# Four small reorderings in a spectral filter fused with a feed-forward layer: x's split, a DFT, a weight buffer and the first PSUM pools

## The chip, the cores and the metric

The kernel runs on one core of a Trainium2 chip. The metric is the device time of one launch in microseconds (us); the times given are medians of several runs. Engines are named as in the profile: PE is TensorE (PEld its weight loads), DVE is VectorE, ACT is ScalarE, POOL is GpSimd, and SP issues every DMA from one queue in order. Each engine works through its own instructions in the order in which the program issues them.

## The reference

Eight batches of 3008 x 256 are transformed along the sequence, mixed by a complex linear layer, shrunk towards zero and transformed back; the result, as 24064 tokens, passes a feed-forward layer of width 2048 with the activation h - tanh(h).

```python
X = np.fft.rfft(x, axis=1)
Yr = Xr @ w_r - Xi @ w_i + b_r
Yi = Xr @ w_i + Xi @ w_r + b_i
Yr = np.sign(Yr) * np.maximum(np.abs(Yr) - lam, 0.0)      # the same for Yi, lam = 0.01
y = np.fft.irfft(Yr + 1j * Yi, n=x.shape[1], axis=1)
h = y.reshape(B * S, D) @ w_in                            # w_in 256 x 2048
out = (h - np.tanh(h)) @ w_out                            # w_out 2048 x 256
```

## The kernel before

**Precision.** Most operands are kept as a high and a low part (hi rounded to the fp32r format by ACT, lo the difference, by POOL or DVE): `split_into`, line 87 for ACT's cast and 88 for the subtraction. A product is then three matmuls: low x high, high x high, high x low. So a matmul group needs its second operand's low half only at its third step.

**The transforms.** 3008 = 64 x 47, so each DFT is done in two steps with a trip through DRAM between them. `Forward` does the first step: `load` brings a piece of x, `split` (a cast x_h on ACT, a subtraction x_l on POOL), `part` (three matmuls, lines 216 to 218, and a copy `st` on ACT that a DMA stores to `a`). `Spectrum` does the rest for a pair of frequencies: `load` reads `at` from `a`; `dft` (line 262) is the second DFT step, with two copies on ACT and two operations on DVE; `shared` and `cross` are the linear layer's products into `ps_t` and `ps_v` (line 289); `join` makes `tb` from `ps_t` (line 300) and then `y` from `tb` and `ps_v` (line 326); `shrink` is the shrinkage; `inverse` (lines 336 to 338) the first step back, with a copy `zo` on ACT that is stored to `z`. `Unit` reads `zin` from `z` and does the last step (line 428) into `raw`, a chunk of 512 or 480 tokens.

**The feed-forward layer.** Chunks 0 to 2 go through `rise`/`fall` directly (H or he, line 481; down, line 505). From chunk 3 on, w_in's product is done as a seven-product 2 x 2 scheme: `Pair` computes two of 16 feature blocks at a time into H in four phases, from sums of weights (`sums`, made once by `weight_sums`) and from sums of halves of the chunk (`sums` and `operands` of `Chunk`; names t1 to t4 and b11 to b22; tiles `y_t`, `y_b`, and `y_more` for b22 and t4). DVE's `u3` (line 592) and `low_right` (line 598) work inside H between the phases. Then tanh (607), the difference (610), the split into gh (614) and gl (618), and the product with w_out (505).

**Order.** All five engines follow the order written in the program (`manual_schedule`). From chunk 3 on a period Q handles one Pair; it has two slots, sa = 46 + 2Q and sb = 47 + 2Q, into which everything else is planned ahead of time. An event in a slot has a rank; `run(slot)` issues them in order of rank, then of insertion. What an event returns is issued later (`run_later`, `run_last`, in the next period's beginning or after the slot). Ranks before: 0 loads, 1 `operands`, 2 `Forward.split`, `shrink` (which only returns its work) and `inverse`, 3 `cross`, 4 `shared`, 6 `dft`, 7 `Forward.part`, 8 `Unit.time`, 9 `Chunk.sums` and `weight_step`.

For a chunk whose first period begins at slot zs, `prepare` puts the operands t3, b11, t2 and b21 into slot zs-3, t1 into zs-2, b22 and t4 into zs-1. Batch 1's spectrum starts at slot 56 with a new pair every 2 slots: dft at k, shared and cross at k+1, shrink at k+2, inverse at k+4. So from slot 60 to 78 every even slot holds one pair's dft and another pair's inverse. Other batches have a pair every 6 slots, and their dft and inverse fall into slots of different parity. The first DFT step of batch b from 2 on is put into the 16 calmest of 20 slots, `split` one slot ahead of its `part`. The weight sums take four steps for each of four parts, in slots 36 to 43 and 46 to 53.

**PSUM** has eight banks. At the start there are three pools: ps_h (2 banks), ps_o (2) and ps_f (4). They are closed together, and ps_oo (2), ps_ff (2) and ps_e (4: he0, he1, oe0, oe1) take their banks in this order. `bank(...)` gives a bank of ps_f first, of ps_ff from then on; from that point ps_f1, ps_f2, ps_t1, ps_v, ps_i1 and ps_i2 all come from its two banks. A new pool waits for the readers and writers of the old pools that lie under it, unless it is opened with `reuse_waits="tile"`, in which case each tile waits only for those under the tile. Later ps_H (two tiles of two banks) takes the banks of ps_e in that way.

Of the kernel before, what the change touches and what calls it, by code (L numbers as in the profile page):

```python
# [10 lines left out]
F32 = mybir.dt.float32  # L11
# [3 lines left out]
ALU = mybir.AluOpType  # L15
# [6 lines left out]
def index_maps():  # L22
    n = np.arange(S)
    time = np.zeros((64, 47), np.int64)
    time[n % 64, n % 47] = n
    starts = []
    for j in range(NJ):
        low = (47 * np.arange(64) + 64 * j) % S < S // 2
        starts.append(next(m for m in range(64) if low[m] and not low[m - 1]))
    return time, starts  # L30
# [36 lines left out]
def spectral_ffn(ctx, tc, x, w_r, w_i, b_r, b_i, w_in, w_out, f1, f2, i1, i2, out):  # L67
    nc = tc.nc
    P = 128
    w_in, w_out = w_in.bitcast(U32), w_out.bitcast(U32)  # L70
    _, m0 = index_maps()
    CT = 512
    NF = FF // P
    PSUM = bass.MemoryType.PSUM
# [3 lines left out]
    work = ctx.enter_context(tc.tile_pool(name="work", bufs=2))  # L78
    ffn = ctx.enter_context(tc.tile_pool(name="ffn", bufs=2))
    dram = ctx.enter_context(tc.tile_pool(name="dram", bufs=2, space=bass.MemoryType.DRAM))  # L80
    start = ExitStack()
    ps_h = start.enter_context(tc.tile_pool(name="ps_h", bufs=2, space=PSUM))
    ps_o = start.enter_context(tc.tile_pool(name="ps_o", bufs=1, space=PSUM))
    ps_f = start.enter_context(tc.tile_pool(name="ps_f", bufs=4, space=PSUM))

    def split_into(hi, lo, src, rest=nc.gpsimd):
        nc.scalar.copy(out=hi, in_=src)  # L87
        rest.tensor_tensor(out=lo, in0=src, in1=hi.bitcast(F32), op=ALU.subtract)  # L88
        return hi, lo
# [149 lines left out]
    def rows(t, jp):  # L239
        return t.rearrange("a (g j) d -> a g (j d)", j=NJ)[:, :, 2 * jp * D:(2 * jp + 2) * D]  # L240

    class Spectrum:
# [98 lines left out]
        def put(self, pz):  # L341
            zo = work.tile([P, 512], F32, name="zo", tag="tmp", bufs=4)
            nc.scalar.copy(out=zo, in_=pz)
            nc.sync.dma_start(out=rows(z_dram[self.b], self.jp), in_=zo)
# [60 lines left out]
    def h(t):  # L405
        return t.bitcast(F32)
# [215 lines left out]

    def weight_sums(p):
        wv = [w.rearrange("p k (q i m) -> p k i q m", i=2, m=P)[:, :, :, 2 * p:2 * p + 2] for w in (win_h, win_l)]
        t = [work.tile([P, 2, P], F32, name=f"ws{k}", tag="tmp", bufs=4) for k in range(3)]

        def whole(dst, k, i):
            nc.vector.tensor_tensor(out=dst, in0=h(wv[0][:, k, i]), in1=h(wv[1][:, k, i]), op=ALU.add)

        def op(dst, a, b, how):  # L630
            nc.vector.tensor_tensor(out=dst, in0=a, in1=b, op=how)

        def put_sum(i, src):
            split_into(*(v[:, 2 * p * P:(2 * p + 2) * P].rearrange("p (q m) -> p q m", m=P) for v in sums[i]), src)

        def one():
            whole(t[0], 0, 1)
            whole(t[2], 0, 0)
            whole(t[1], 1, 1)

        def two():
            op(t[1], t[0], t[1], ALU.add)
            op(t[0], t[2], t[0], ALU.subtract)
            put_sum(2, t[0])

        def three():
            put_sum(0, t[1])
            op(t[1], t[1], t[2], ALU.subtract)
            whole(t[2], 1, 0)

        def four():
            put_sum(1, t[1])
            op(t[2], t[2], t[1], ALU.subtract)
            split_into(wv[0][:, 0, 1], wv[1][:, 0, 1], t[2])

        return one, two, three, four

    slots = {}
# [4 lines left out]
    later = [[], []]  # L663

    def run(slot):
        for _, _, fn, a in sorted(slots.pop(slot, []), key=lambda e: e[:2]):
            later[0].extend(fn(*a) or ())

    def run_later():
# [18 lines left out]
    def busy(slot, us):  # L688
        load_at[slot] = load_at.get(slot, 0.0) + us

    def plan_spectrum(b, at, each, offsets, ahead, earliest):
        shared, cross, shrink, inverse = offsets
        done_at[b] = at + (NJ // 2 - 1) * each + inverse
        for jp in range(NJ // 2):
            s = Spectrum(b, jp)
            k = at + jp * each
            put(max(k - ahead, earliest), 0, s.load)
            for slot, rank, fn, us in (
                (k, 6, s.dft, 1.8), (k + shared, 4, s.shared, 0.7), (k + cross, 3, s.cross, 1.4),
                (k + shrink, 2, lambda s=s: [s.shrink], 0.3), (k + inverse, 2, s.inverse, 0.7),  # L700
            ):
                put(slot, rank, fn)
                busy(slot, us)
            if shared == cross:
                busy(k + shared, 9.0)

    def plan_forward(f, q, slot):
        put(slot - 1, 2, f.split, q)
        put(slot, 7, f.part, q)
        busy(slot, 0.8)  # L710
        busy(slot - 1, 0.1)
# [21 lines left out]
    def plan():  # L733
# [8 lines left out]
        for ch in range(LOOK, NP // XC):  # L742
            k = ch - LOOK
            f = following[ch]
            put((40, 41, 44, 47, 48, 49)[k], 0, f.load)
            for q in range(XC // 2):
                plan_forward(f, q, 47 + k)
        plan_spectrum(1, 56, 2, (1, 1, 2, 4), 5, 53)
        for b in range(2, B):
            zs = zero_slot(b * WB_N)  # L750
            plan_spectrum(b, zs - 89, 6, (2, 3, 4, 7), 7, zs - 92)
        for b in range(2, B):
            zs = zero_slot(b * WB_N)
            at = calmest(zs - 113, zs - 94, NP // 2, 0.8)
            for ch in range(NP // XC):
                f = Forward(b, ch)
                put(at[2 * ch] - 5, 0, f.load)
                for q in range(XC // 2):
                    plan_forward(f, q, at[2 * ch + q])
# [13 lines left out]
    def weight_step(p, k):  # L773
        if not sums:
            sums.extend([piece(i + 3 * v, [P, FF // 2], F32R, f"sum{i}_{v}") for v in range(2)] for i in range(3))
        if k == 0:
            wsteps[p] = weight_sums(p)
        wsteps[p][k]()
# [27 lines left out]
    with tc.manual_schedule(engines={E.PE, E.Activation, E.DVE, E.Pool, E.SP}):  # L806
# [24 lines left out]
        for i in range(len(steps) + 2):  # L831
# [9 lines left out]
            if i >= 2:  # L841
                f, q = steps[i - 2]
# [120 lines left out]
        ps_ff = ctx.enter_context(tc.tile_pool(name="ps_ff", bufs=2, space=PSUM))  # L963
        banks[0] = ps_ff
        first_pass = ExitStack()
        ps_e = first_pass.enter_context(tc.tile_pool(name="ps_e", bufs=1, space=PSUM))
        early_h = [ps_e.tile([P, 512], F32, name=f"he{k}", tag=f"he{k}") for k in range(2)]
        early_o = [ps_e.tile([P, 512], F32, name=f"oe{k}", tag=f"oe{k}") for k in range(2)]
        H = []
# [35 lines left out]
        for g in range(-AHEAD, LAST):  # L1005
            rise(g + AHEAD)
            if g < CONV:
                early(g)
                if g == CONV - 1:
                    some(80)  # L1010
                    assert raw_count == 16 and not any(pending) and not any(streams)
                    plan()
            else:
                run(g)
                run_later()
                run_last()
            finish(g + AHEAD)
            for t in range(2):
                fall(g, t)
# [14 lines left out]
        for Q in range(-1, PERIODS + 2):  # L1034
# [13 lines left out]
            call(Q + 1, "keep")  # L1048
            run_last()
            run(sa)  # L1050
            run_later()
            finish(sa + AHEAD)
# [10 lines left out]
            fall(sb, 0)  # L1063
            call(Q - 1, "down", 0, 0)
            run(sb)
            fall(sb, 1)
            call(Q - 1, "down", 0, 1)
# [34 lines left out]
```

## Time and profile before

| | |
|---|---|
| median of 3 runs | 2660.9 us (2659.74 to 2662.64) |
| profiled execution | 2656.65 us; span from first to last instruction 2654.8 us |
| PE busy | 2611.6 us, 98% |
| DVE, ACT, POOL busy | 65%, 59%, 26% |
| mean granted PE clock | 0.994 |
| HBM read and written | 86.13 and 74.97 MB |

The span less PE's busy time is the time in which PE stood still. A row of the wait list names who waited, for whom, for how long in total, how often, and the longest time. In the timeline a row gives start and duration in us, engine, line, operation, the tile written and the tiles read, how many instructions were merged, and in brackets the idle time ahead of it and what ended it. A merged row's duration reaches to the end of its last matmul; matmuls overlap, so the next one starts before.

### The profile page before, as it was taken

How to read it: one execution, taken by the hardware profiler on the slowest of the kernel's cores; microseconds unless marked ns; L12 is line 12 of the kernel's file. 1: busy time of each engine (PE TensorE's matmuls, PEld its weight loads, DVE VectorE, ACT ScalarE, POOL GpSimd, SP SyncE). 2: the span in 40 equal slices, each digit the busy share in tenths (PEclk: the TensorE clock that was granted, in tenths of full speed). 3: DMA queues.
4: the chain of work that ended last, by engine and by line, in shares of the span. 5: the costliest groups of instructions: out<-in, count | busy, mean ns of one | idle time of the engine just before them, and what ended most of it. 6: DMA issues, size and time to landing. Idle time of an engine off the chain costs nothing.

```text
span 2654.8 us, 43312 instructions
## 1 busy us (share of the span) xinstructions
PE 2611.6 (98%) x16641; PEld 2343.2 (88%) x16641; DVE 1720.6 (65%) x2613; ACT 1578.9 (59%) x2950; POOL 697.9 (26%) x829
## 2 busy tenths in 40 slices
PE   8999999999999999999999999999999999999999
PEld 6787788899989999899998999989999899999998
DVE  6787676576656667466664666646665566665655
ACT  5555656655566555755566555665556655555555
POOL 0002524322242222512334232332223322221210
PEclk8899999999999999999999999999999999999999
DMA  6420313211131111311114011231112211111000
GB/s 195 149 76 14 110 59 102 70 40 53 38 111 55 47 50 40 106 59 40 45 49 125 29 54 38 73 95 41 43 52 84 68 46 55 36 33 33 16 24 16
DMA packets 104654, 163.90 MB, mean 62 GB/s; under 512 B 8000, under 2 KB 62272, under 8 KB 104352
## 3 DMA queue, kind: packets, MB, share of 16 engines
q1 hardware_dynamic: 104448, 161.13, 19.7%
q8 instruction: 132, 2.16, 0.3%
q14 instruction: 74, 0.61, 0.1%
HBM read 86.13 MB, written 74.97 MB: 61 GB/s over the span
## 4 chain that ended last, share of the span: by engine, by line
PE 86%; DVE 2%; POOL 1%; ACT 1%; issue 1%; DMA 0%; SPq 0%; POOLq 0%; ACTq 0%; DVEq 0%
PE o L505 36%; PE H L576 32%; PE ps_v L289 4%; PE ps_i L428 4%; PE ps_f L262 3%; PE ps_t L289 2%; PE ps_f L218 1%; PE ps_f L216 1%; PE ps_f L217 1%; DVE y L326 1%; PE ps_i L336 1%; PE ps_i L337 1%; PE ps_i L338 1%; POOL x_l L88 1%; DVE tb L300 0%
## 5 line engine op out<-in xcount | busy, mean ns | idle before, releaser
L576 PEld LDWEIGHTS H<-y_t,sum 128*128 128x128 f32 x3240 | 530.6, 188 | 91.8 <-DVE H L592 3.9
L505 PE MATMUL o<-gh,wout_l 128*128 128x512 f32 (+1 forms) x1440 | 572.5, 398 | 0.1
L505 PE MATMUL o<-gh,wout_h 128*128 128x512 f32 (+1 forms) x1440 | 561.5, 390 | 0.0
L505 PE MATMUL o<-gl,wout_h 128*128 128x512 f32 (+1 forms) x1440 | 560.7, 389 | 0.5 <-DVE gl L618 0.5
L576 PE MATMUL H<-y_t,sum 128*128 128x256 f32 (+1 forms) x3240 | 550.9, 278 | 4.1 <-DVE H L592 3.5
L614 ACT CAST gh<-th 128x1024 fp32r<-128x1024 f32 (+1 forms) x360 | 372.3, 1034 | 281.1 <-DVE th L610 231.4
L618 DVE TENSOR_TENSOR gl<-th,gh 128x1024 fp32r<-128x1024 f32 (+1 forms) x360 | 435.7, 1210 | 48.8 <-ACT gh L614 44.1
L592 DVE TENSOR_TENSOR H<-H,late 128x256 f32<-128x256 f32 (+1 forms) x360 | 153.6, 427 | 450.5 <-PE H L576 407.7
L610 DVE TENSOR_TENSOR th<-H,th 128x1024 f32<-128x1024 f32 (+1 forms) x360 | 429.3, 1192 | 2.4 <-ACT th L607 0.3
L607 ACT ACTIVATE th<-H 128x1024 f32<-128x1024 f32 (+1 forms) x360 | 364.6, 1013 | 108.8 <-PE H L576 105.7
L505 PEld LDWEIGHTS o<-gl,wout_h 128*128 128x128 f32 x1440 | 270.3, 188 | 56.1 <-DVE gl L618 0.9
L88 POOL TENSOR_TENSOR z_l<-mn,z_h 128x512 fp32r<-128x512 f32 x84 | 110.3, 1313 | 769.3 <-ACT z_h L87 769.3
L598 DVE TENSOR_TENSOR H<-H,late 128x256 f32<-128x256 f32 (+1 forms) x360 | 153.6, 427 | 242.1 <-PE H L576 235.7
L576 PE MATMUL H<-y_b,win_h 128*128 128x256 f32 (+1 forms) x1440 | 284.7, 279 | 0.0
L505 PEld LDWEIGHTS o<-gh,wout_l 128*128 128x128 f32 x1440 | 272.1, 189 | 6.8 <-ACT gh L614 0.5
L505 PEld LDWEIGHTS o<-gh,wout_h 128*128 128x128 f32 x1440 | 272.0, 189 | 5.7
L584 ACT COPY late<-H 128x256 f32<-128x256 f32 (+1 forms) x360 | 132.8, 369 | 235.5 <-PE H L576 232.6
L576 PE MATMUL H<-y_more,win_h 128*128 128x256 f32 (+1 forms) x1440 | 266.5, 278 | 0.0
L576 PEld LDWEIGHTS H<-y_more,win_h 128*128 128x128 f32 x1440 | 219.0, 189 | 4.4
L576 PEld LDWEIGHTS H<-y_b,win_h 128*128 128x128 f32 x1440 | 219.6, 189 | 0.0
L576 PE MATMUL H<-y_more,win_l 128*128 128x256 f32 (+1 forms) x720 | 209.3, 291 | 0.0
L576 PE MATMUL H<-y_b,win_l 128*128 128x256 f32 (+1 forms) x720 | 200.8, 279 | 0.0
(173 smaller groups left out, 4213.6 us busy)
## 6 DMA issues: line engine op xcount, KB each, us to landing
xt<-in_x SPq DMA_DIRECT2D x64, 384.0 KB, 3.8
at<-a SPq DMA_DIRECT2D x96, 256.0 KB, 3.2
z<-zo SPq DMA_DIRECT2D x96, 256.0 KB, 2.1
a<-st SPq DMA_DIRECT2D x56, 384.0 KB, 3.4
zin<-z SPq DMA_DIRECT2D x58, 288.0 KB, 3.8
out<-ot SPq DMA_DIRECT2D x32, 512.0 KB, 3.1
out<-ot SPq DMA_DIRECT2D x16, 480.0 KB, 3.4
zin<-z SPq DMA_DIRECT2D x31, 192.0 KB, 3.6
```

The source lines that it names most:

```text
L88: rest.tensor_tensor(out=lo, in0=src, in1=hi.bitcast(F32), op=ALU.subtract)
L289: nc.tensor.matmul(dst, lhs[:, t], rhs[:, t, :], start=n == 0, stop=n == 5)
L428: nc.tensor.matmul(ps[:, k * 94:(k + 1) * 94], self.zt[:, k, t * P:(t + 1) * P], i2t[:, (self.p + k) * 94:(self.p + k + 1) * 94], start=Tr ...
L505: nc.tensor.matmul(self.o[t][:, :n], lhs[:, f, t * P:(t + 1) * P], rhs, start=f == 0 and k == 0, stop=f == NF - 1 and k == 2,)
L576: nc.tensor.matmul(dst, a, b, start=start and k == 0, stop=k == 2, skip_group_check=True)
L584: nc.scalar.copy(out=self.p7, in_=self.c11)
L592: nc.vector.tensor_tensor(out=self.c21, in0=self.acc, in1=self.p7, op=ALU.add)
L598: nc.vector.tensor_tensor(out=self.c22, in0=self.acc, in1=self.p7, op=ALU.add)
L607: nc.scalar.activation(out=self.th, in_=self.hp[:, :, :n], func=AF.Tanh)
L610: nc.vector.tensor_tensor(out=self.th, in0=self.hp[:, :, :self.n], in1=self.th, op=ALU.subtract)
L614: nc.scalar.copy(out=self.gh, in_=self.th)
L618: nc.vector.tensor_tensor(out=self.gl, in0=self.th, in1=h(self.gh), op=ALU.subtract)
```

## The change

Four edits. (1) ps_f is opened first among the starting pools, so that it lies on the first four banks, and ps_e is opened with `reuse_waits="tile"`. (2) `weight_sums` has four buffers, as halves of two tiles, instead of three tiles; the third step writes its difference into the new one instead of over its operand. (3) `inverse` gets rank 2.5, and `run` puts it behind `dft` (rank 6.5) in a slot that holds both and nothing of rank 3, 4, 7 or 8. (4) `Forward.split` gets rank 0.5, ahead of `operands`.

```diff
@@ spectral_ffn
     start = ExitStack()
+    ps_f = start.enter_context(tc.tile_pool(name="ps_f", bufs=4, space=PSUM))
     ps_h = start.enter_context(tc.tile_pool(name="ps_h", bufs=2, space=PSUM))
     ps_o = start.enter_context(tc.tile_pool(name="ps_o", bufs=1, space=PSUM))
-    ps_f = start.enter_context(tc.tile_pool(name="ps_f", bufs=4, space=PSUM))
...
@@ weight_sums
-        t = [work.tile([P, 2, P], F32, name=f"ws{k}", tag="tmp", bufs=4) for k in range(3)]
+        pair = [work.tile([P, 2, 2, P], F32, name=f"ws{k}", tag="tmp", bufs=4) for k in range(2)]
+        t = [v[:, k] for v in pair for k in range(2)]
...
         def three():
             put_sum(0, t[1])
-            op(t[1], t[1], t[2], ALU.subtract)
+            op(t[3], t[1], t[2], ALU.subtract)
             whole(t[2], 1, 0)
 
         def four():
-            put_sum(1, t[1])
-            op(t[2], t[2], t[1], ALU.subtract)
+            put_sum(1, t[3])
+            op(t[2], t[2], t[3], ALU.subtract)
             split_into(wv[0][:, 0, 1], wv[1][:, 0, 1], t[2])
...
     def run(slot):
-        for _, _, fn, a in sorted(slots.pop(slot, []), key=lambda e: e[:2]):
+        events = slots.pop(slot, [])
+        ranks = {e[0] for e in events}
+        if ranks >= {2.5, 6} and not ranks & {3, 4, 7, 8}:
+            events = [(6.5, *e[1:]) if e[0] == 2.5 else e for e in events]
+        for _, _, fn, a in sorted(events, key=lambda e: e[:2]):
             later[0].extend(fn(*a) or ())
...
@@ plan_spectrum
-                (k + shrink, 2, lambda s=s: [s.shrink], 0.3), (k + inverse, 2, s.inverse, 0.7),
+                (k + shrink, 2, lambda s=s: [s.shrink], 0.3), (k + inverse, 2.5, s.inverse, 0.7),
...
@@ plan_forward
-        put(slot - 1, 2, f.split, q)
+        put(slot - 1, 0.5, f.split, q)
...
-        ps_e = first_pass.enter_context(tc.tile_pool(name="ps_e", bufs=1, space=PSUM))
+        ps_e = first_pass.enter_context(tc.tile_pool(name="ps_e", bufs=1, space=PSUM, reuse_waits="tile"))
```

## The prediction

> **What bounds the kernel now.** I read the busy times first, then TensorE's own list of waits, then a table of stretches, and last the timeline at each place the waits name.
>
> ```profile
> span 2654.8 us, 43312 instructions
> PE 2611.6 (98%) x16641; PEld 2343.2 (88%) x16641; DVE 1720.6 (65%) x2613; ACT 1578.9 (59%) x2950; POOL 697.9 (26%) x829
> ...
> PE ps_f L218 <- POOL x_l L88: 9.8, 7, 1.6
> PE ps_f L262 <- DVE y L326: 7.2, 10, 0.7
> PE H L576 <- DVE H L592: 3.5, 1, 3.5
> ...
> 320.00:440.00 120.00, 111.58 (x743) 99.67 (x744) 88.40 (x150) 67.52 (x132) 44.92 (x48) 1.00 0.19 62
> ...
> 2200.00:2500.00 300.00, 300.00 (x1989) 274.73 (x1988) 191.57 (x269) 174.43 (x324) 68.67 (x89) 1.00 0.11 35
> ```
>
> TensorE (PE) is busy for 2611.6 of 2654.8 us. The table's columns are the stretch, its length, then busy time and count of PE, weight load, DVE, ACT and POOL, the granted clock, DMA share and GB/s. From 2200 to 2500 PE is busy for 300.00 of 300 us at clock 1.00: such a stage has nothing left to remove; 320 to 440 lacks 8.4 us. The change takes no matmul away, so all it can win lies in 2654.8 - 2611.6 = 43.2 us of idle PE, plus what half-clock stretches cost. The wait rows (total, times, longest) name three kinds of place; two single ones stand below. Each part of the diff points at one or two of them. I take them in order of time. A stall's cost is counted from where PE would have issued its next matmul; that is a little more than the listed wait, since a matmul's end lies behind the next one's start.
>
> **PSUM pools in another order, ps_e by tile.**
>
> ```profile
> 108.57 9.09 PE L428 MATMUL ps_i<-i,zin 96*128 96x94 f32 x48 [1.14 <-DMA zin<-z]
> 119.28 1.19 PE L481 MATMUL he<-yh,win_l 128*128 128x512 f32 x2 [1.62 <-DVE yl L462]
> ...
> 114.59 0.30 DVE L462 TENSOR_TENSOR yl<-ps_i,yh 128x136 fp32r<-128x136 f32 x1 [0.46 <-ACT yh L461]
> ...
> 123.00:125.00 2.00, 2.00 (x12) 1.72 (x11) 1.23 (x2) 1.15 (x2) 0.00 (x0) 0.77 0.00 0
> ```
>
> The inverse's 48 matmuls end at 108.57 + 9.09 = 117.66. The first he needs chunk 0's yl, whose last piece (136 columns) ends at 114.59 + 0.30 = 114.89, yet it starts at 119.28: the banks under ps_e are ps_f's, and the pool waits for every reader of ps_f. With ps_f allocated first, ps_e lies on the banks of ps_h and ps_o, which were last used long before, and waits tile by tile. So he starts at 117.66 and the stall of 1.62 us goes. What gets ps_f's banks instead is ps_oo and ps_ff; ps_ff's first user comes behind two he groups (some 5 us at this clock), when those readers are through: nothing. PE runs at half clock here until about 123.9 (a mean of 0.77 from 123 to 125 is half clock for 2 x 0.23 / 0.5 = 0.92 us). I take **-1.6 us**: the clock rises as long after he's start as now. Bounds: -0.8 (it still rises at 123.9, so the time won is spent at half clock) and -1.62 - (123.9 - 119.28) / 2 = -3.9 (no half clock left from he on).
> Row against rule: "TensorE: Matmul & The Clock Gate", Part 1, of the Trainium skill has the clock decided in free-running windows of about 3.4 us. By it the rise stays near 123.9 or comes a window sooner, an estimated 0.8 or 2.5 us where the rows alone give 1.6; the sum below would be 15.6 or 17.3.
>
> **Fourth buffer for weight sums.** Three DVE operands become four in two tiles of 2 KB instead of three of 1 KB in slots of the same tag; no instruction is added. The third step writes t[3] instead of t[1] in place, so it no longer waits for GpSimd (POOL) to read t[1]. First place:
>
> ```profile
> 252.56 0.94 DVE L631 TENSOR_TENSOR ws<-ws,ws 128x256 f32<-128x256 f32 x1 [1.82 <-POOL sum L88]
> ...
> 252.89 0.40 PE L505 MATMUL oe<-ghe,wout_h 128*128 128x512 f32 x1
> 253.13 0.39 PE L505 MATMUL oe<-gle,wout_h 128*128 128x512 f32 x1
> 255.22 0.73 PE L481 MATMUL H<-yh,win_l 128*128 128x512 f32 x2 [1.70 <-DVE the L485]
> ...
> 257.57 0.58 ACT L516 COPY ot<-oe 128x512 f32<-128x512 f32 x1
> ...
> 258.25 0.59 PE L576 MATMUL H<-y_t,sum 128*128 128x256 f32 x3 [0.65 <-POOL y_b L88]
> ```
>
> DVE's wait of 1.82 us pushes th (L485) and with it the first matmul on H: 1.70 us. PE could have issued at 253.13 + 0.24 (the spacing of the two rows before it) = 253.37, so 1.85 us are lost. Without the wait th comes about 1.6 us sooner, by an estimate from the 1.82 less what its own tanh then holds it, so some 1.5 us come back. The second stall (0.65) I leave standing: the tile H1 lies on the oe banks, whose copy by ScalarE (ACT) ends at 257.57 + 0.58 = 258.15 behind the queue that the same th feeds, so it moves along. **-1.5 us**, bounds -0.8 and -2.5. Second place:
>
> ```profile
> 272.55 1.51 DVE L618 TENSOR_TENSOR gl<-th,gh 128x1024 fp32r<-128x1024 f32 x1 [0.48 <-ACT gh L614]
> 277.19 1.48 DVE L631 TENSOR_TENSOR ws<-ws,ws 128x256 f32<-128x256 f32 x1 [3.13 <-POOL sum L88]
> 278.71 2.05 DVE L628 TENSOR_TENSOR ws<-win_h,win_l 128x256 f32<-128x256 f32 x1
> 280.68 0.42 DVE L592 TENSOR_TENSOR H<-H,late 128x256 f32<-128x256 f32 x1
> ...
> 273.78 2.68 POOL L88 TENSOR_TENSOR x_l<-xt,x_h 94x512 fp32r<-94x512 f32 x2 [0.80 <-ACT x_h L87]
> 276.43 0.73 POOL L88 TENSOR_TENSOR sum<-ws,sum 128x256 fp32r<-128x256 f32 x1
> ...
> 277.28 0.39 PE L505 MATMUL o<-gl,wout_h 128*128 128x512 f32 x1
> 281.15 1.01 PE L576 MATMUL H<-y_t,sum 128*128 128x256 f32 x3 [3.48 <-DVE H L592]
> ...
> 282.00:284.00 2.00, 2.00 (x8) 1.71 (x8) 0.92 (x4) 1.35 (x2) 0.73 (x1) 0.50 0.23 82
> ```
>
> DVE is free at 272.55 + 1.51 = 274.06 but waits 3.13 us for POOL's sum, queued behind two x_l; then two weight operations, L592, and only then PE's next matmul, which would have issued at 277.28 + 0.24 = 277.52: 3.63 us lost. The clock then stands at 0.50 from 281.15 to about 284.2, another (284.2 - 281.15) / 2 = 1.5 us. With t[3] the two operations start at 274.06. At their slow durations here (1.48 + 2.05, both beside x_l on POOL) they end at 277.59, L592 at 278.0, and PE loses 0.5 us; at the 0.42 us of L592's like they end before 275 and it loses none. I take 0.25 and no half clock: 3.63 + 1.5 - 0.25 = **-4.9 us**, bounds -4.6 and -5.1 (0 if the wait stays). What is late next: POOL, with two x_l of 1.3 us for each slot.
> A rule that speaks against this part stands in the Trainium skill's "SBUF — State Buffer", Who interferes with whom: a DVE operation with two SBUF inputs and a POOL operation that reads SBUF shut each other out for a whole instruction. The slow 1.48 and 2.05 beside x_l agree; by it both operations must sit behind the x_l pair again, the residue is the full 0.5 us, and the sum below would be 16.1.
>
> **Batch 1's second DFT ahead of the inverse.** The condition holds in slots 60, 62, 72, 74, 76 and 78; 64 to 70 hold an inverse-time unit (rank 8) and 80 a forward part.
>
> ```profile
> 406.25 0.47 PE L336 MATMUL ps_i<-z_h,i_l 128*128 128x512 f32 x1
> ...
> 406.78 0.40 PE L338 MATMUL ps_i<-z_l,i_h 128*128 128x512 f32 x1
> 407.90 1.16 PE L262 MATMUL ps_f<-f,at 128*128 128x128 f32 x8 [0.72 <-DVE y L326]
> 408.82 0.36 PE L576 MATMUL H<-y_more,win_l 128*128 128x240 f32 x1
> ...
> 405.42 0.68 DVE L300 TENSOR_TENSOR tb<-ps_t,bias 128x512 f32<-128x512 f32 x1
> 406.13 1.71 DVE L326 TENSOR_TENSOR y<-tb,ps_v 64x256 f32<-64x256 f32 x4
> ```
>
> Two banks serve both. The first to ask gets ps_t's, free at 405.42 + 0.68 = 406.10; the second gets ps_v's, free when y ends at 407.84. The inverse never waits and the DFT always does, ten times. Swapped, the DFT takes the early bank and the inverse the late one: the wait changes hands. DFT 406.25 to 407.17 (its 0.92 from 407.90 to 408.82), then until 407.90 nothing, then the inverse's 0.77 (406.78 + 0.24 - 406.25) to 408.67, against 408.82: 0.15 us each, 6 x 0.15 = **-0.9 us**. If the inverse did not wait, it would be the whole gap, 6 x 0.88 = -5.3; if the DFT still waits, 0. On ACT the DFT's copies now precede zo; zo's store comes later by up to their 1 us, slots ahead of its use.
>
> **Split of x ahead of the y operands.** It moves x_h on ACT and x_l on POOL past the operand casts; no DMA is issued by either. Only four-operand slots matter: one for each of batches 2 to 7, six in all; this is one of them.
>
> ```profile
> L88 POOL TENSOR_TENSOR x_l<-xt,x_h x108: 1261/1293/2195, 266.6 to 2083.0; 94x512 fp32r<-94x512 f32 x108
> ...
> 788.54 0.40 ACT L87 CAST y_t<-late 128x256 fp32r<-128x256 f32 x1
> ...
> 789.76 0.62 ACT L87 CAST x_h<-xt 94x512 fp32r<-94x512 f32 x1
> ...
> 789.01 0.74 POOL L88 TENSOR_TENSOR y_t<-late,y_t 128x256 fp32r<-128x256 f32 x1 [1.50 <-PE H L576]
> ...
> 791.79 2.19 POOL L88 TENSOR_TENSOR x_l<-xt,x_h 94x512 fp32r<-94x512 f32 x1
> ...
> 791.62 1.25 DVE L618 TENSOR_TENSOR gl<-th,gh 128x960 fp32r<-128x960 f32 x1 [0.53 <-ACT gh L614]
> ...
> 791.59 0.39 PE L576 MATMUL H<-y_b,win_h 128*128 128x256 f32 x2
> ...
> 794.03 0.48 PE L218 MATMUL ps_f<-x_l,f_h 94*96 94x512 f32 x1 [1.58 <-POOL x_l L88]
> ```
>
> Now POOL works off four y operands (0.7 us apart from 789.01) before x_l, which ends at 793.98 and holds L218 for 1.58 us (1.75 from where PE would have issued it). After: x_h from 788.54 to 789.16, x_l at its median 1.29 from 789.23 to 790.52, y_t to 791.24, b11's y_b to 791.95. PE wants x_l only at 794.03 - 1.75 = 792.28: that wait goes. But it wants b11's low half at 791.59 + 0.12 = 791.71: a new stall of 0.3 us. The other two operands then run into gl (L618), beside which x_l took 2.19 instead of 1.29, and POOL is 1.3 us later for the rest of the new chunk's operands; PE needs these between 0.2 and 1 us after I have them ready. I put 0.2 us for that: 1.75 - 0.3 - 0.2 = 1.25, 6 x 1.25 = **-7.5 us**. Bounds: -10.5 if y_b is in time, and if x_l ahead also takes 2.19 and y_b then sits behind gl, b11 comes at about 793.8, a stall of 2.1, six times +0.4 = +2.4.
>
> Where split and inverse share a slot, zo goes 0.62 us later, ahead of a wait for z that is four slots away: nothing. Rank 2.5 against 2 only passes shrink, which issues later anyway.
>
> **Sum:** 1.6 + 1.5 + 4.9 + 0.9 + 7.5 = 16.4 us. The profiled execution took 2656.65 us (span 2654.8), so 2640.3 for its like. The median of the runs shown, 2660.9, is 4.25 us above it; 2660.9 - 16.4 = **2644.5 us**.
>
> **Rivals.**
> - *The stall changes engine.* In the four-operand slots y_b comes as late as x_l did. For: POOL's queue holds the same work; against: y_b needs only one x_l more ahead of it. Split gives 0: gain 8.9, 2652 us.
> - *Nothing is late next.* Both weight waits go whole (2.5 + 5.1), y_b is in time (10.5), the start 1.6 and the swap 0.9: 20.6, so 2640.3; 2635.9 if the inverse does not wait either (5.3 for 0.9). For: PE waits for none of the operands now; against: y_b's 0.3 us follows from durations alone.
> - *It doesn't do what it says.* Writes to one half of a pair tile wait for POOL's reads of the other half, so the weight stall (6.4) returns one step on, and the split trades: gain 2.5, 2658.4. Against: POOL and ACT write parts of the tile late side by side now.
> - *Slower.* A delayed y_b idles PE so long that the clock halves, as at 281. It decides from a stall of 1.75 + 8.9 / 6 = 3.2 us at each of six places; at 3.6 with 1.5 of half clock behind, 6 x (5.1 - 1.75) = 20.1, less 8.9: +11.2, 2672 us. It needs POOL 3 us later than the rows make it.
>
> **How the numbers follow.** Forecast 0.56 (its own range 2641 to 2649), nothing late next 0.15, stall changes engine 0.16, doesn't do what it says 0.09, slower 0.04. A measurement of this kernel tells about 0.2% (5.3 us) from no change, so faster 0.87 (the first three), same 0.09, slower 0.04. The range 2637 to 2653 reaches the second and third cases and leaves out the rest.
>
> **What would show it.** Right: no wait of PE on x_l near 790 and every 320 us after; he at 117.7; no gap or half clock at 277 to 284; L336 waiting for y in six slots, L262 in four. Wrong: PE waiting on y_t, y_b or y_more in those slots for more than 1 us; L631 still waiting for POOL; the DFT still waiting in all ten.

## The result, and the profile after

| | before | after |
|---|---|---|
| median | 2661.08 us (2659.74 to 2662.64, 4 runs) | 2639.64 us (2637.5 to 2642.25, 4 runs) |
| profiled execution | 2656.65 us, span 2654.8 | 2641.14 us, span 2639.3 |
| mean granted PE clock in it | 0.994 | 0.995 |

The ratio is 0.9924 with an interval of 0.9912 to 0.9935: 21.4 us faster, where 16.4 were forecast. The two profiled executions lie only 15.5 us apart: that of before is 4.4 us below its median, that of after 1.5 us above its own. Most of the experiments below serve to explain those 6 us. First the page of the changed kernel and its list of waits (total, times, longest):

```profile
span 2639.3 us, 43323 instructions
PE 2608.5 (99%) x16641; PEld 2342.9 (89%) x16641; DVE 1729.1 (66%) x2613; ACT 1579.1 (60%) x2950; POOL 700.9 (27%) x829
```

```profile
PE ps_i L336 <- DVE y L326: 3.4, 6, 0.6
...
PE ps_f L262 <- DVE y L326: 2.9, 4, 0.7
...
PE ps_i L428 <- ACT st L230: 2.2, 2, 1.7
...
PE ps_f L218 <- POOL x_l L88: 1.0, 2, 0.5
```

The waits for x_l fall from 9.8 us to 1.0, the weight sums' 3.5 us (H behind L592) are gone from the list, and the wait for y has changed hands in six of ten slots. New is a wait of 1.7 us for `st`. The kernel before has this at the same place:

```profile
294.22 0.91 PE L428 MATMUL ps_i<-i,zin 96*128 96x94 f32 x6 [0.16 <-ACT st L230]
```

In the timeline of the changed kernel, PE at the four places of the change, in order of time:

```profile
107.54 8.65 PE L428 MATMUL ps_i<-i,zin 96*128 96x94 f32 x48 [1.72 <-DMA zin<-z]
115.90 1.20 PE L481 MATMUL he<-yh,win_l 128*128 128x512 f32 x2
...
250.13 0.73 PE L481 MATMUL H<-yh,win_l 128*128 128x512 f32 x2 [0.23 <-DVE the L485]
253.15 0.60 PE L576 MATMUL H<-y_t,sum 128*128 128x256 f32 x3 [0.66 <-POOL y_b L88]
...
271.46 0.47 PE L218 MATMUL ps_f<-x_l,f_h 94*96 94x512 f32 x1 [0.49 <-POOL x_l L88]
280.27 0.47 PE L218 MATMUL ps_f<-x_l,f_h 94*96 94x512 f32 x1 [0.49 <-POOL x_l L88]
286.25 0.91 PE L428 MATMUL ps_i<-i,zin 96*128 96x94 f32 x6 [1.67 <-ACT st L230]
...
783.59 0.74 PE L576 MATMUL H<-y_b,win_h 128*128 128x256 f32 x2
784.64 0.39 PE L218 MATMUL ps_f<-x_l,f_h 94*96 94x512 f32 x1
```

At the start he follows the inverse with nothing between. Near 250 the wait on H has shrunk from 1.70 to 0.23 and the 0.66 behind it stands, as forecast. At 271 to 286 two waits for x_l (before had one, of 0.31) and the one for st have taken the place of the 3.48. In batch 3 the split's L218 runs with no bracket where it waited 1.58.

How much of PE's time each stretch lacks is read from the table of stretches, whose columns are those of the prediction. Of before, the long stretch with batches 3 to 7, and of after this one and the one with the swapped DFTs:

```profile
480.00:2600.00 2120.00, 2112.08 (x13978) 1927.14 (x13977) 1356.17 (x1993) 1278.00 (x2384) 585.43 (x704) 1.00 0.18 54
```

```profile
320.00:440.00 120.00, 112.98 (x751) 101.88 (x752) 87.31 (x147) 69.85 (x131) 42.08 (x44) 1.00 0.23 73
...
480.00:2600.00 2120.00, 2119.61 (x14032) 1935.21 (x14031) 1368.27 (x2002) 1281.40 (x2393) 588.22 (x709) 1.00 0.18 54
```

Idle PE falls from 7.92 to 0.39 us there. The count says the same in another way: 54 more matmuls are through in the same 2120 us, at 2120 / 14032 = 0.151 us each 8.2 us. From 320 to 440 it falls from 8.42 to 7.02.

The same sum over the whole span closes for every kernel run here, with a rest of 2594.3 to 2597.4 us in all 14 profiles. Idle is length less PE's busy time; the loss is length x (1 - clock), added up over stretches of 5 us; the rest is what the matmuls take at full clock.

| profile | span | PE idle | lost to half clock | rest |
|---|---|---|---|---|
| before | 2654.8 | 43.2 | 16.1 | 2595.5 |
| before_again | 2660.1 | 46.9 | 17.8 | 2595.4 |
| split_back | 2652.4 | 41.1 | 15.9 | 2595.4 |
| split_only | 2645.6 | 37.9 | 11.9 | 2595.8 |
| weights_in_place | 2642.9 | 35.5 | 12.0 | 2595.4 |
| after | 2639.3 | 30.8 | 12.1 | 2596.4 |
| after_again | 2635.4 | 31.8 | 7.0 | 2596.6 |
| weights_late | 2636.0 | 30.0 | 10.3 | 2595.7 |
| best | 2630.8 | 29.0 | 6.8 | 2595.0 |

So a microsecond is either idle or a half-clock loss, and both differ between executions of one and the same kernel: the two of the kernel before by 3.7 us of idle time, most of it in the first 130 us, and 1.7 us of half clock, the two of the changed kernel by 1.0 and 5.1 us.

### The profile page after: what moved, and what is told of

Read it like the earlier page. It is cut to its first block, busy times and chain, and to the rows that moved or that the text cites. A ratio compares the mean times of both kernels' runs of the same rounds, so it can differ in the third digit from the quotient of the medians.

```text
span 2639.3 us, 43323 instructions
## 1 busy us (share of the span) xinstructions
PE 2608.5 (99%) x16641; PEld 2342.9 (89%) x16641; DVE 1729.1 (66%) x2613; ACT 1579.1 (60%) x2950; POOL 700.9 (27%) x829
## 4 chain that ended last, share of the span: by engine, by line
PE 93%; DVE 2%; issue 2%; POOL 1%; DMA 1%; ACT 1%; POOLq 0%; SPq 0%; ACTq 0%; DVEq 0%
PE o L505 37%; PE H L576 32%; PE ps_v L289 4%; PE ps_i L428 4%; PE ps_f L262 3%; PE he L481 2%; PE ps_t L289 2%; PE ps_v L371 1%; PE ps_f L216 1%; PE ps_f L218 1%; PE ps_f L217 1%; PE oe L505 1%; DVE y L326 1%; PE ps_i L336 1%; PE ps_i L337 1%
## 5 line engine op out<-in xcount | busy, mean ns | idle before, releaser
L618 DVE TENSOR_TENSOR gl<-th,gh 128x1024 fp32r<-128x1024 f32 (+1 forms) x360 | 443.0, 1231 | 49.3 <-ACT gh L614 44.7
L592 DVE TENSOR_TENSOR H<-H,late 128x256 f32<-128x256 f32 (+1 forms) x360 | 153.6, 427 | 438.5 <-PE H L576 387.8
```

The source lines that it names most:

```text
L592: nc.vector.tensor_tensor(out=self.c21, in0=self.acc, in1=self.p7, op=ALU.add)
L618: nc.vector.tensor_tensor(out=self.gl, in0=self.th, in1=h(self.gh), op=ALU.subtract)
```

## The experiments

The kernel before had medians of 2659.34, 2659.18 and 2660.01 us in the three comparisons; each experiment's ratio is to the one beside it. All but two start from the changed kernel.

**The split of x.** Two kernels and the two repeats. In split_back the one line is undone; split_only is the kernel before with that line alone.

```diff
-        put(slot - 1, 0.5, f.split, q)
+        put(slot - 1, 2, f.split, q)      # split_back; split_only is the reverse, in before
```

> The changed kernel with the split of x back at rank 2, behind the y operands; the other three edits stay. Theory A (the split is worth what its six places show in the changed kernel's trace: 0.75 us at batch 2 and 1.47 at each of five others, 8.1 us): some 8 us above the changed kernel, ratio to before about 0.9955, with PE again waiting 1.6 us for x_l six times. Rival B (the stall only changed engine, the gain comes from elsewhere): within 2 us of the changed kernel, ratio about 0.993.

Measured: 2652.78 us (2649.97 to 2657.14, 9 runs), ratio 0.9974 (0.9965 to 0.9984). The stalls are back in its list of waits:

```profile
PE ps_f L218 <- POOL x_l L88: 10.5, 8, 1.6
```

Against the changed kernel's 2639.64 that is 13 us (11 against its repeat below), more than either theory gave, and more than the stalls' length. So the kernel before was run once more, unchanged.

> The kernel before, unchanged, for its spread and the clock of each run. Theory A (runs differ by how long the clock stays at half after the idle places of the first 300 us): times between 2656 and 2663 that fall as the mean clock rises, ratio 1.000. Rival B (the spread is not the clock's): times without relation to the clock.

Measured: 2660.83 us (2657.99 to 2664.27, 11 runs), ratio 1.0003 (0.9995 to 1.0012). The times fall as the mean clock rises, as theory A said, but not only for what happens in the first 300 us. Its profile has the same six stalls of 1.58 us for x_l as the first one, but what follows them differs. Its stretches, around the stall at 793 and around the one at 1113:

```profile
790.00:795.00 5.00, 3.42 (x20) 2.74 (x19) 2.93 (x4) 3.12 (x7) 5.00 (x6) 1.00 0.33 99
795.00:800.00 5.00, 5.00 (x33) 4.60 (x33) 1.95 (x4) 3.66 (x6) 3.77 (x5) 1.00 0.00 0
...
1110.00:1115.00 5.00, 3.42 (x20) 2.72 (x19) 2.89 (x4) 3.09 (x7) 5.00 (x6) 1.00 0.35 101
1115.00:1120.00 5.00, 5.00 (x23) 4.45 (x22) 1.49 (x2) 2.72 (x6) 3.71 (x5) 0.66 0.00 0
...
480.00:2600.00 2120.00, 2112.08 (x13947) 1926.89 (x13946) 1353.15 (x1990) 1274.15 (x2381) 584.70 (x704) 1.00 0.18 54
```

Both stalls leave 3.42 of 5 us busy. Behind the first the clock stays at 1.00 and 33 matmuls go through in 5 us; behind the second it is 0.66, which is 5 x 0.34 / 0.5 = 3.4 us at half clock, and 23 go through: 1.7 us lost on top of the 1.58. Scanned in steps of 10 us, the six stalls were followed by half clock three times in this execution, twice in split_back's, never in the first one of before: 5 times in 18. In the eleven profiles of kernels without these stalls there is no half clock at all from 440 to 2620 us. In the long stretch before_again got 31 matmuls less done than before with the very same idle time: 4.7 us, about three times 1.7.

> The kernel before with one line of the change: x is split ahead of the y operands (rank 2 to 0.5); PSUM order, weight sums and the order of inverse and DFT stay as they were. Theory A (a stall for x_l of 1.6 us costs its own length in every execution and, in some executions, also a stretch at half clock behind it; the median holds both): the profile shows the six stalls gone and is about 8 us shorter than the profile of before with no half clock behind 791, but the median is 12 to 13 us below the median of before, a ratio of 0.995 to 0.9955, and the runs lie closer together than those of before. Theory B (a stall costs its length and nothing else): 7.5 to 8 us, a ratio of 0.997 to 0.9972. Theory C (the 21 us come from the change's parts together, none of them worth more than its stall): also 0.997.

Measured: 2646.9 us (2646.16 to 2648.1, 5 runs), ratio 0.9951 (0.9939 to 0.9964), as theory A said: 13.1 us from one line. The interval reaches from 9.6 to 16.2 us, which leaves out theory B's 8. Its long stretch has the idle time of the changed kernel:

```profile
480.00:2600.00 2120.00, 2119.59 (x14026) 1934.66 (x14025) 1367.64 (x2001) 1281.94 (x2395) 589.68 (x710) 1.00 0.18 54
```

The mean clock of its five runs is 0.995 to 0.996, that of the kernel before beside it 0.992 to 0.994. Their medians, 0.995 and 0.993, differ by 0.002 x 2650 = 5.3 us, and with the 7.5 us of idle time in this stretch that makes 12.8; the clocks are known to 0.001 only, which is 2.7 us. That the runs lie closer together is not shown: they span 1.9 us against 5.6, but without its slowest run the kernel before spans 1.9 too.

> The changed kernel once more, nothing altered. Theory A: a median of 2638 to 2641 us, a ratio of 0.992 to 0.9932 with a narrower interval, and a profile whose stalls are the same to 0.1 us; what differs between its two profiles are stretches at half clock alone. Theory B (the first comparison of the change was favoured by chance, and it is worth the 15.5 us that lie between the two first profiles): 2645 us, 0.9942.

Measured: 2641.88 us (2637.2 to 2643.08, 5 runs), ratio 0.9928 (0.9916 to 0.9941): 18.1 us. The ratio is within theory A's, the median 0.9 us above it and 3 us below B's. From 240 us on the stalls are the same to 0.1 us, as theory A said, but not ahead of it: near 110 the first profile waits 1.72 us for `zin`, the second 1.64 for a copy on DVE. The wait for st is 1.64 after 1.67 us. That wait in after_again's timeline, the stretch behind it in the same execution, and the stretch behind it in the changed kernel's first profile:

```profile
284.00 0.91 PE L428 MATMUL ps_i<-i,zin 96*128 96x94 f32 x6 [1.64 <-ACT st L230]
```

```profile
286.00:290.00 4.00, 4.00 (x27) 3.55 (x25) 2.32 (x4) 2.28 (x5) 1.27 (x3) 1.00 0.39 101
```

```profile
288.00:290.00 2.00, 2.00 (x8) 1.71 (x8) 0.00 (x0) 1.02 (x1) 0.70 (x1) 0.50 0.51 140
```

The changed kernel's first profile pays for the same stall with half clock, that of after_again does not. Seven of the profiles, some of them taken up below, have this wait for st, of 1.64 to 1.86 us; five of them lose 1.7 us to half clock behind it (after, split_back, pools_back, b11_first, xl_on_dve), two do not (after_again, no_swap). The shorter span of after_again, 2635.4 for 2639.3, comes from half clock alone (12.1 to 7.0 us in the table above); idle time is 1 us longer. The larger part, 3.4 of the 5.1 us, lies near the start, in the first profile and then in the second:

```profile
105.00:130.00 25.00, 23.29 (x124) 20.50 (x123) 15.48 (x32) 11.55 (x27) 0.00 (x0) 0.80 0.53 139
```

```profile
105.00:130.00 25.00, 22.70 (x134) 19.42 (x133) 17.34 (x36) 12.34 (x32) 0.00 (x0) 0.93 0.52 139
```

**The weight sums.** First the third step writes over t[1] again.

```diff
-            op(t[3], t[1], t[2], ALU.subtract)
+            op(t[1], t[1], t[2], ALU.subtract)
             ...
-            put_sum(1, t[3]); op(t[2], t[2], t[3], ALU.subtract)
+            put_sum(1, t[1]); op(t[2], t[2], t[1], ALU.subtract)
```

> The changed kernel with the third weight step writing over its operand again (two tiles stay). Theory A (the fourth buffer is worth 1.4 us at its first place and 1.3 at the second, since a stall and a half clock come back ten microseconds later): 2.5 to 3 us above the changed kernel, ratio about 0.9935, PE waiting 3.5 us for L592 near 270 and not for ACT's st copy near 284. Rival B (the forecast's 6.4 us, the late stall being chance): 6 us or more above, ratio 0.995, and the st wait unchanged.

Measured: 2644.71 us (2643.23 to 2646.03, 5 runs), ratio 0.9942 (0.9928 to 0.9956): 5.1 us above the changed kernel's first median and 2.8 above its second, with intervals that overlap. In the trace the stall is back, and the wait for st is down to 0.15 us:

```profile
278.38 1.01 PE L576 MATMUL H<-y_t,sum 128*128 128x256 f32 x3 [3.47 <-DVE H L592]
```

So the wait for st is what came in place of this one. Why st is late stands in the timelines of ACT, POOL and DVE in the changed kernel:

```profile
283.69 0.41 ACT L87 CAST sum<-ws 128x256 fp32r<-128x256 f32 x1 [1.85 <-DVE ws L632]
284.00 1.04 ACT L614 CAST gh<-th 128x1024 fp32r<-128x1024 f32 x1
284.95 0.36 ACT L584 COPY late<-H 128x256 f32<-128x256 f32 x1
285.34 0.36 ACT L585 COPY H<-H 128x256 f32<-128x256 f32 x1
285.61 1.07 ACT L230 COPY st<-ps_f 96x512 f32<-96x512 f32 x2
...
277.32 5.59 POOL L88 TENSOR_TENSOR x_l<-xt,x_h 94x512 fp32r<-94x512 f32 x4
...
276.69 3.81 DVE L629 TENSOR_TENSOR ws<-win_h,win_l 128x256 f32<-128x256 f32 x3
...
281.89 1.30 DVE L632 TENSOR_TENSOR ws<-ws 128x256 f32<-128x256 f32 x1
283.23 0.42 DVE L632 TENSOR_TENSOR ws<-ws,ws 128x256 f32<-128x256 f32 x1
```

ACT stands idle 1.85 us ahead of the cast of the last part's sum, waiting for DVE, and behind that cast queue gh, two copies and only then st. DVE is late since its weight operations take up to 1.3 us beside x_l on POOL, where 0.42 is their length alone. ACT's order is the same in the kernel before, but there the stall moved the same three operations into a pause between POOL's x_l, and they took 1.09 us instead of 3.81:

```profile
285.12 1.09 DVE L628 TENSOR_TENSOR ws<-win_h,win_l 128x256 f32<-128x256 f32 x3
```

Two explanations were to be told apart: x_l holds DVE up, or the weight part is badly placed. xl_on_dve lets DVE do batch 1's x_l, so that POOL's x_l and DVE no longer meet; weights_moved puts the third and fourth part elsewhere.

```diff
-        put(slot - 1, 0.5, f.split, q)
+        put(slot - 1, 0.5, f.split, q, None, nc.vector if f.b == 1 else nc.gpsimd)   # xl_on_dve
...
-        for p, at in enumerate((36, 40, 46, 50)):
+        for p, at in enumerate((36, 40, 44, 52)):      # weights_moved; weights_late: 36, 40, 46, 52
```

> The changed kernel with the low half of batch 1's split x computed by DVE instead of POOL. Theory A (POOL's x_l and DVE's weight operations shut each other out between 264 and 285 us, which holds ACT's queue and through it PE's next bank): the weight operations go down to 0.42 us each, PE's waits for x_l and st there and the half clock behind them go, 3 us below the changed kernel, ratio 0.991. Rival B (DVE itself is full there): PE waits for L592 or gl instead, no gain or a loss.

Measured: 2641.96 us (2638.71 to 2644.9, 5 runs), ratio 0.9933 (0.992 to 0.9945). PE's waits for x_l are gone and the weight operations are down to 0.42 us, but the wait for st stays, and ACT's cast still waits 1.42 us for DVE. PE's row, then two of DVE's:

```profile
286.72 0.91 PE L428 MATMUL ps_i<-i,zin 96*128 96x94 f32 x6 [1.86 <-ACT st L230]
...
282.06 1.28 DVE L88 TENSOR_TENSOR x_l<-xt,x_h 94x512 fp32r<-94x512 f32 x2
283.26 0.41 DVE L632 TENSOR_TENSOR ws<-ws 128x256 f32<-128x256 f32 x1
```

The two x_l now stand in DVE's own queue, right ahead of L632, and take 1.28 us, as long as the slow L632 did. So this run does not settle the question: it puts one delay of DVE in the other's place.

> The changed kernel with the weight sums' third and fourth parts begun at slots 44 and 52 instead of 46 and 50, so that the fourth lies behind batch 1's splits of x. Theory A (DVE's weight operations and POOL's x_l shut each other out and hold ACT's queue, whence the 1.67 us wait for st and the half clock behind it): that wait and the half clock go, some 3 us below the changed kernel, ratio 0.991. Rival B (POOL alone is too slow for two x_l a slot, whatever DVE does): PE still waits 1.5 us or more in all for x_l and st between 265 and 290, time within 1 us of the changed kernel.

Measured: 2640.75 us (2637.55 to 2641.66, 5 runs), ratio 0.9925 (0.9912 to 0.9937): no gain. From 280 to 300 PE is not idle and the clock is 1.00, but the third part, two slots earlier, makes a new wait at 262:

```profile
262.25 0.36 PE L576 MATMUL H<-y_more,win_l 128*128 128x256 f32 x1 [1.14 <-ACT sum L87]
```

So only the fourth part was moved next.

> The changed kernel with the last of the four weight sums two slots later (slots 36, 40, 46, 52 in place of 36, 40, 46, 50), nothing else. Theory A (PE's wait of 1.67 us for st at 286.25 comes from ACT's queue, in which the copy of the last weight sum waits 1.85 us for DVE ahead of gh, the H copies and st): the wait for st goes with the half clock behind it, the waits of weights_moved at 259 and 262 do not come, and the profile is 1.7 to 3.5 us shorter than that of the changed kernel: 2637 to 2638 us, a ratio of 0.991 to 0.992 to the kernel before. Theory B (st is late for another reason, the split of x on POOL beside DVE): the wait stays within 0.3 us and the time is that of the changed kernel, 0.9925.

Measured: 2639.0 us (2636.18 to 2642.03, 5 runs), ratio 0.9924 (0.991 to 0.9937), 2.9 us below after_again, less than these intervals can separate. The profile is clear: the wait for st at this place is gone, no wait comes at 262, and the stretch is full but for 0.18 us.

```profile
280.00:300.00 20.00, 19.82 (x127) 17.16 (x126) 12.28 (x20) 14.09 (x30) 6.00 (x7) 1.00 0.37 104
```

```profile
284.33 1.09 DVE L629 TENSOR_TENSOR ws<-win_h,win_l 128x256 f32<-128x256 f32 x3
```

So the fourth weight part, at its place, is what makes st late: moved by two slots, it takes the wait away. This also takes its operations out from beside x_l (1.09 us for the three again). By the rows above they lost 3.81 - 1.09 = 2.7 us there and L632 another 0.9, more than the 1.85 that ACT waited, so the slowness beside x_l is the likely way in which the place does it; no run changes it alone.

**The PSUM pools and the swap.** pools_back opens ps_f last again and ps_e without `reuse_waits`; no_swap leaves out the condition in `run`.

```diff
-    ps_f = start.enter_context(tc.tile_pool(name="ps_f", bufs=4, space=PSUM))      # pools_back
     ps_h = ...
     ps_o = ...
+    ps_f = start.enter_context(tc.tile_pool(name="ps_f", bufs=4, space=PSUM))
...
-        if ranks >= {2.5, 6} and not ranks & {3, 4, 7, 8}:
-            events = [(6.5, *e[1:]) if e[0] == 2.5 else e for e in events]      # no_swap
```

> The changed kernel with the first PSUM pools in their old order and ps_e waiting for the whole of ps_f. Theory A (the edit takes 1.6 us of PE's wait ahead of the first he, and up to a second of half clock): 1.5 to 3 us above the changed kernel, ratio about 0.993, he again 1.6 us or more behind the inverse's last matmul. Rival B (the wait is only moved to ps_ff's first user): the same time as the changed kernel.

Measured: 2642.96 us (2640.65 to 2646.33, 5 runs), ratio 0.9939 (0.9927 to 0.9952), 1.1 to 3.3 us above the changed kernel, again with overlapping intervals. In the trace he waits again:

```profile
115.03 1.19 PE L481 MATMUL he<-yh,win_l 128*128 128x512 f32 x2 [1.90 <-DVE yl L462]
```

The four profiles without this edit (before, before_again, split_only and this one) all have the wait, of 1.62 to 3.00 us, the ten with it none. Whether it also saves half clock is open: between 109 and 124 the four lose 3.4 to 6.8 us, the ten 1.7 to 5.1.

> The changed kernel without the swap of DFT and inverse in batch 1. Theory A (the wait for y only changes hands): 0.9 us above the changed kernel, which this measurement can hardly tell from it (ratio 0.9925 to 0.993), and in the trace ten waits of 0.72 us of L262 for y and none of L336. Rival B (the swap is worth the whole gap): 5 us above, ratio 0.9945.

Measured: 2639.49 us (2638.97 to 2642.32, 5 runs), ratio 0.9927 (0.9914 to 0.9941): not to be told from the changed kernel by its time. The waits of the kernel before are back, ten for L262, none for L336, and so is the idle time:

```profile
PE ps_f L262 <- DVE y L326: 7.2, 10, 0.7
```

```profile
320.00:440.00 120.00, 111.55 (x740) 99.37 (x738) 85.15 (x144) 67.87 (x130) 40.47 (x43) 1.00 0.24 74
```

8.45 us idle against 7.02 in the first profile of the changed kernel (8.15 in the second, where the stretch begins elsewhere in the work).

**The operands that PE needs first.** b11_first keeps t3 and b11 ahead of the split and puts t2 and b21 behind it; best is that together with weights_late.

```diff
-        put(at - 3, 1, chunk.operands, "t3", "b11", "t2", "b21")
+        put(at - 3, 0.25, chunk.operands, "t3", "b11")
+        put(at - 3, 1, chunk.operands, "t2", "b21")
```

> The changed kernel with t3 and b11 put ahead of the split of x and only t2 and b21 behind it. Theory A (b11's low half, late by 0.35 us in six slots, is what is left there; x_l is not needed for 2 us after): six times 0.35 us less, some 2 us below the changed kernel, ratio 0.9915, and PE's y_b matmuls in those slots back at 0.39 us for two. Rival B (x_l then comes late again behind two operands): waits for x_l of 0.5 us or more in the six slots, no gain.

Measured: 2640.39 us (2637.61 to 2642.64, 5 runs), ratio 0.9927 (0.9914 to 0.9939): no gain that the time shows. The trace has one:

```profile
480.00:2600.00 2120.00, 2120.00 (x14042) 1936.44 (x14041) 1369.12 (x2004) 1282.31 (x2394) 588.45 (x709) 1.00 0.18 54
```

Ten matmuls more than the changed kernel in the same stretch, 10 x 0.151 = 1.5 us, or 0.3 for each of the five places. This wait stands in no list, since it is hidden in a merged row: the two y_b matmuls at 783.59 took 0.74 us in the changed kernel, where 0.39 is usual.

> The changed kernel with the last weight sum two slots later and with only the operands t3 and b11 ahead of the split of x, t2 and b21 behind it. Theory A: the wait for st goes (1.7 us and up to 1.8 us of half clock) and so do the hidden-operand waits of batches 3 to 7 (0.39 us in all between 480 and 2600 us): 2636 to 2638 us, a ratio of 0.9905 to 0.992. Theory B (both places are taken over by waits of other work): 2639 to 2641 us, 0.9925.

Measured: 2634.8 us (2632.61 to 2637.03, 4 runs), ratio 0.9905 (0.9892 to 0.9919), 1.2 us below what theory A expected. Its slowest run is faster than the fastest of after_again beside it (2637.2). The two edits explain 1.5 + 1.7 us and, where half clock follows the wait for st, 1.7 more; against after_again the gain is 7.1, against the first median of the changed kernel 4.8, so at most some 2 us of it are left unexplained. Both places read as full:

```profile
280.00:300.00 20.00, 20.00 (x136) 17.93 (x136) 13.49 (x21) 12.82 (x27) 4.63 (x7) 1.00 0.31 90
...
480.00:2600.00 2120.00, 2120.00 (x14044) 1936.78 (x14043) 1370.03 (x2005) 1281.10 (x2394) 587.23 (x709) 1.00 0.18 53
```

## Why the prediction was right, and where it was not

The direction, the places and four of the five mechanisms came as written. The time, 2639.64, lies just outside the forecast's own 2641 to 2649 and is the one that *nothing is late next* gave (2640.3), but not for that rival's reason: things are late next, at the places below, and another term was larger. The sum is in part luck: between the two profiles 15.5 us are gained, close to the 16.4, but one term is 3.6 too large and others, among them 1.0 us by which the first inverse happened to begin sooner, make up for most of it.

| part | forecast | shift between the two profiles | timed, edit alone or undone |
|---|---|---|---|
| PSUM pools | 1.6 | 1.6 of stall; 2.35 up to he | 1.1 to 3.3 |
| weight sums, first place | 1.5 | 1.43 | |
| weight sums, second place | 4.9 | 1.34 | 2.8 to 5.1, both places |
| DFT ahead of the inverse | 0.9 | 0.97 | not measurable |
| split of x | 7.5 | 8.1 | 13.1 alone, 10.9 to 13.1 undone |

- **PSUM pools, right.** he starts right behind the inverse, though at 115.90 and not at 117.7: the inverse itself began 1.03 us sooner and ran 0.44 us shorter. Nothing shows that the change did this; the two profiles of the kernel before differ by as much there (108.57 and 107.07). The shift from the first L428 to he is 3.38 - 1.03 = 2.35 us, of which those 0.44 are a part.
- **Weight sums, first place, right** to 0.1 us, with the second stall of 0.65 left standing as written (0.66).
- **Weight sums, second place: the step that failed.** 3.63 + 1.5 - 0.25 took the stall away and asked only what DVE does next; the shift is 1.34, outside the bounds of 4.6 and 5.1. The sentence "What is late next: POOL, with two x_l" named the two waits of 0.49 but gave them no price, and what stands behind the stall in the queues was not followed: without it DVE reaches the fourth part while POOL is still at its x_l, the three operations take 3.81 us instead of 1.09, ACT's cast waits for them, and st stands behind that cast. Two times 0.49 and 1.67 of the 3.63 are lost again, and in the first profile 1.7 us of half clock too, as much as before. The rule of the Trainium skill's "SBUF — State Buffer", Who interferes with whom, that such operations of DVE and POOL shut each other out agrees with the slow operations (1.30 beside x_l, 0.42 alone). The prediction applied it only to the two operations right behind the stall: these were slow (1.51 and 1.39 us), but PE waited for L592 no longer.
- **DFT ahead of the inverse, right:** six waits for L336, four for L262, 0.97 us between the instructions at 320 and 428. Only the trace shows it.
- **Split of x: right in mechanism, mis-sized.** For batches 3 to 7 the shift is 1.47 us each, for batch 2 0.75. The forecast for each place was 1.75 - 0.3 - 0.2: the 0.3 for b11 is there (b11_first gets it back), the 0.2 for the other operands did not come. What the sum did not hold is the half clock that follows some of these stalls. The profile that was argued from had none behind any of the six, so 1.58 looked like the whole price, and its 4.25 us below the median were carried over unchanged to the forecast. They should not have been: the second profile of the kernel before has three such half clocks, 5.1 us, which go with the stalls. 5 of 18 stalls x 1.7 us is 0.5 for each, some 3 us for a run; the timed difference asks for 5 (interval 1.5 to 8). That the six stalls bring the half clocks is shown by split_only and split_back together; how often they do is known only that roughly.

Of the other rivals, *the stall changes engine* and *slower* fell with PE's list of waits: no listed wait on y_t, y_b or y_more is above 0.7 us. *It doesn't do what it says* fell with the wait of L631, which is gone.

## What to carry to other kernels

Before a stall is put down as gone, follow every in-order queue past the instruction that it held back, ACT's copies too: work that is released early can meet other work that slows it, and hold up something behind it that PE wants sooner; in the trace, moving that one piece by two slots took the new wait away. Take the price of a stall from several executions, not from one profile: here a stall near 1.6 us cost its length every time and sometimes as much again in clock. Where a median lies above the profiled execution, ask which places make up the gap before adding it to both sides.

## What was not expected of the hardware

Six stalls of the same length in the same program, 1.58 us, were followed by 3.4 us at half clock in 5 of 18 cases and by none in the others; of the seven waits of 1.64 to 1.86 us for st, five were, and the changed kernel had it in one execution and not in the next. That makes part of the spread of one kernel's runs: before_again ran from 2657.99 us at a mean clock of 0.994 to 2664.27 at 0.992.

The half clock comes in equal pieces. Added up over stretches of 1 or 2 us, every half-clock stretch before 2600 us in the 14 profiles costs 1.7, 3.4, 5.1 or 6.8 us, so it lasts one, two, three or four times 3.4 us (four times in the first profile of the kernel before, from 110 to 124). The Trainium skill, "TensorE: Matmul & The Clock Gate", Part 1, describes a window of about 3.4 us that runs freely, not started by the kernel; the length of the half clock here agrees, and chance in where a stall falls within such a window would explain that some are followed by it, which no run here isolates. The same page's section "Why this matters for your kernels" advises against idle gaps of more than about 3 us; here gaps of half that were sometimes enough, so the measurement sets the shorter bound.
